# Windowed attention with sinks and a squared-relu layer on one core: order of the first scores, who masks them, and who turns one x

## The chip, the cores and the metric

The kernel runs on one core of a Trainium2 chip. A core has five engines that run side by side and wait for each other through semaphores: TensorE (PE, matmuls and transpositions, writes to PSUM), VectorE (DVE), ScalarE (ACT), GpSimd (POOL) and SyncE (SP, which issues DMAs here; POOL and ACT issue some too). PSUM is used as four score-sized banks, so an operation of TensorE may wait for a bank. The metric is the device time of one execution in microseconds. Before the change it is 226.25 us in the median of four runs (225.96 to 226.46).

## The reference

```python
scores = scale * np.matmul(q, k.transpose(0, 1, 3, 2))       # (4, 8, 768, 768), head_dim 64
keep = is_sink | in_window                                   # first 4 keys; 0 <= i - j < 128
scores = np.where(keep, scores, -1000000000.0)
a = np.exp(scores - np.max(scores, axis=-1, keepdims=True))
a = a / (np.sum(a, axis=-1, keepdims=True) + 1e-09)
attn_out = np.matmul(a, v)
x = attn_out.transpose(0, 2, 1, 3).reshape(B * S, H * D)     # (3072, 512)
h = x @ w_in                                                 # (3072, 2048)
out = np.maximum(h, 0.0) ** 2 @ w_out                        # (3072, 512)
```

## The kernel before

There are four batches of 768 tokens. A batch is cut into three s of 256 tokens (s = 0, 1, 2) and six tiles t of 128; its eight heads go in four pairs m. For each batch attention makes x, layer 1 (`layer1`, L684 to L711) multiplies it with w_in and squares the relu, layer 2 (`layer2`, L714 to L774) multiplies with w_out and stores.

**Attention** (`attention`, its inner `stage`). In batches 0 and 1 SP loads fp32 queries and keys (`qr`, L348), in two groups of tokens: g = 0 holds tokens 0 to 511, g = 1 the last 256. They are cast and regrouped to `qs` (`regroup`), turned by TensorE into PSUM (`transpose`, pt, L476) and copied to `qkT` by VectorE and ScalarE (`unload`). Batches 2 and 3 (`NATURAL`) are cast by POOL's loads (`qn`, L380) and turned by DMA transposes on SP (L436). For each s, `scores` (ps) multiplies a block of 128 keys with up to 256 queries in the window; ScalarE takes the exponential (`expo`, expm, L590); a mask removes what lies outside the window; `values` (po, L634) multiplies with v, whose 65th column sums the weights, and adds the sinks (`es`, `vs`); `norm` divides (L645, L646) into `xn_sb`; `bridge` turns the result by TensorE (px, L671) and a copy makes `xT`. In batches 2 and 3 that turn is made by two DMA transposes per s on SP (`turn_x`, L657) instead.

**Masks.** Three ways stand in the code. With `biased` (batch 0 and s < `BIASED` = 2) TensorE first writes a bias of -30000 outside the window into the bank, as a product with the identity (`bias0` for s = 0, `bias` for s = 1, L564), and adds the scores to it, so that the exponential gives zero. Otherwise VectorE multiplies expm with a 0/1 tile (`mask0` for s = 0, `mask` for the rest, L599), or POOL cuts triangles. `mask` and `mask0` are copied together from two triangles `tri` by POOL (`build_masks`, L252).

**Order.** The order of each engine is not that of the source. Every operation is handed to a planner (`Plan`) with a key, a cost for each engine that may do it, and what it follows; the planner puts them one after the other by earliest start and then key, and the program is written in that order. Each engine then runs its own in order. Costs, `PE_SLACK`, the `margin` of a DMA, and the keys (`at(...)`, `LO`, `HI`) only steer this order. DMAs on one queue are issued in their order; `behind` makes an issue wait for the landing of a named load. SP issues batch 0's first queries and keys (pairs 0 to 3, key before query), the last ones of batch 0 behind the landing of the first part of w_out, and batch 1's behind batch 0's last v. POOL issues v, the four parts of w_in, w_out, later v and the `qn` loads. PSUM banks come from two pools, `att` and `den`, of two each; layer 1 and layer 2 take from `den` alone. `warm` fills expected waits of TensorE in the first 34 us with dummy transpositions (L201).

Around the change TensorE runs, in batch 0: transpositions, then the scores of s = 0 and s = 1 in turns by pair, the four values, both turns of x, and then the eight blocks of layer 1 (four blocks of features, s = 0 and s = 1 in turns). In batch 1 it takes s = 2 first, then s = 0 and s = 1.

Of the kernel before, what the change touches and what calls it, by code (L numbers as in the profile page):

```python
# [14 lines left out]
ALU = mybir.AluOpType  # L15

LATENCY = 0.2
PE_SLACK = 0.334
DMA_START = {"sp": 1.2, "act": 1.2, "pool": 1.6}
DMA_LATENCY = 0.9  # L20
WARM_UNTIL = 34.0
# [112 lines left out]
def kernel(  # L134
# [11 lines left out]
    nc = tc.nc  # L146
# [102 lines left out]
        nc.gpsimd.tensor_copy(out=bias0, in_=bias)  # L249
        nc.gpsimd.memset(bias0[0:NSINK, 1:3, :], 0.0)  # L250

    def build_masks(e):  # L252
        for h2 in range(2):
            for i in range(2):
                nc.gpsimd.tensor_copy(out=mask[:, h2, 2 * i:2 * i + 2, :], in_=tri)
                nc.gpsimd.tensor_copy(out=mask0[:, h2, 2 * i:2 * i + 2, :], in_=tri)
            nc.gpsimd.memset(mask0[0:NSINK, h2, 1:3, :], 1.0)

    def build_head_rows(e):

# [6 lines left out]

    c_fill = op(-9, {"dve": 2.5}, fill)
    c_ident = op(-9, {"pool": 0.3}, build_ident)
    c_tri = op(-0.15, {"pool": 0.6}, build_triangles)  # L270
    c_bias = op(-8, {"pool": 1.3}, build_bias)
    c_sinks = op(-7, {"pool": 0.5}, build_head_rows)


    loaded = {}
# [92 lines left out]
    def load_natural(b, s, older_values):  # L368

        begun = [ops["layer1", b - 2, 0, 0], w_out_op[3]]  # L370
        for ti in (1, 0):
            if s == 0:
                qn_slot[b, ti] = Slot("qr", NT)
            for i in range(2):
                t = 2 * s + i

                def run(e, t=t, ti=ti):
                    if t == 0:
                        qn_t[b, ti] = work["qr"].tile([128, NT, DM], BF16, name="qn", tag="qr")
                    return [nc.gpsimd.dma_start(  # L380
                        out=qn_t[b, ti][:, t, :].rearrange("p (h d) -> p h d", d=D),
                        in_=(q, k)[ti][b, :, 128 * t:128 * t + 128, :].rearrange("h p d -> p h d"))]
                o = dma_op("pool", ("qk", b, ti, t), run, 64 * 0.032,
                           None,
                           [qn_slot[b, ti]] if t == 0 else ())
                o.after += begun
                o.margin = 1.661
        for t in (2 * s, 2 * s + 1):
            def run(e, t=t):
                return [nc.gpsimd.dma_start(  # L390
                    out=v_sb[b % 2][:, t, :, 0:D],
                    in_=v[b, :, 128 * t:128 * t + 128, :].rearrange("h p d -> p h d"))]
            o = dma_op("pool", ("v", b, t), run, 64 * 0.032)
            o.after += begun + older_values
            o.margin = 1.661

    def load_sinks(queue, b):
        eng = nc.scalar if queue == "act" else nc.sync
# [3 lines left out]
    def attention(b, key):  # L402
# [16 lines left out]
        def stage(g, f0, f1, side):  # L419
# [4 lines left out]
            def at(f):  # L424
                return key(f0 + (f1 - f0) * f)
# [3 lines left out]
            if b in NATURAL:  # L429
                for s in range(NS):  # L430
                    for ti in (1, 0):
                        for i in range(2):
                            t = 2 * s + i

                            def turn(e, s=s, ti=ti, i=i, t=t):
                                nc.sync.dma_start_transpose(  # L436
                                    out=qkT_sb[:, :, ti, t, :], in_=qn_t[b, ti][:, t, :])
                            ops["turn", b, ti, t] = op(
                                at(0.1 * s), {"sp": 1.25}, turn, dma=0.3, reads=[qn_slot[b, ti]],
                                after=[ops["qk", b, ti, t]] + prev_scores + prev_sinks)  # L440
                            ops["turn", b, ti, t].margin = 5.167
                            copies.append(ops["turn", b, ti, t])
                    ops["cast", b, s] = ops["v", b, 2 * s + 1]
            w = 2 if n == 2 else 1
# [100 lines left out]
            for s in range(t0 // 256, last // 256):  # L545
# [3 lines left out]
                for m0 in (0, 2):  # L549
# [24 lines left out]
                                        rhs=qkT_sb[r, m, 0, qb:qb + w // 128, :],  # L574
                                        start=(i == 0 and not biased), stop=(i == len(segs) - 1))
                    sc = []
                    for ms in ((m0,), (m0 + 1,)) if b == 0 else ((m0, m0 + 1),):
                        sc.append(op(
                            at(fm), {"pe": len(ms) * (0.7 if biased else 0.28) + 0.1}, lambda e, f=scores, ms=ms: f(e, ms),
                            takes=[banks[m - m0] for m in ms],  # L580
                            after=[ops["turn", b, ti, t] for ti in (0, 1)
                                   for t in range(max(0, 2 * s - 1), 2 * s + 2)] if b in NATURAL else
                            [c for m in ms for gg in range(g + 1) for c in ops["copies", b, m, gg]]))
                        ops["scores", b, s, ms[0]] = sc[-1]
                    masked = []
                    o = 0 if s else 128
                    for j, m in enumerate((m0, m0 + 1)):
# [19 lines left out]
                        if biased:  # L607
                            masked.append(ex)
                            continue
                        first = b == 0 and s < 2  # L610
                        masked.append(op(at(fm + 0.03), {"pool": 1.3} if first else
                                         {"pool": 1.3, "dve": 0.7} if s else {"dve": 0.58, "pool": 1.1},
                                         domask, after=[ex] if first else [ex, late["masks"]]))

                    bo = Slot(side, 1)

# [37 lines left out]
                if b in NATURAL or b == 1 and s in TURNED:  # L654
                    for t in (2 * s, 2 * s + 1):
                        def turn_x(e, t=t):
# [146 lines left out]
    load_v(1, 1, None, ())  # L803
    load_v(1, 2, None, ())

    LO, HI = 0.12, 0.624
    for b in range(B):
        if b == 0:
            at = attention(0, lambda f: f - 1.0)
            at(0, 0.0, 1.0, ("den", "att"))  # L810
            late["masks"] = op(0.006, {"pool": 3.0}, build_masks, after=[c_tri, ops["bridge", 0, 1]])
            at(1, 0.2, 0.725, "att")
        if b == 0:
            for i in range(4):
                for s in range(2):
                    layer1(b, 0.083 * i + 0.042 * s, range(4 * i, 4 * i + 4), 256 * s, 256, (s,))
        else:
            for i, fb in enumerate(range(0, NFB, 2)):
                layer1(b, b + 0.34 * i / 8, (fb, fb + 1), 0, 512, (0, 1))
        for i, fb in enumerate(range(0, NFB, 4)):  # L820
            if b == 0:
                layer1(b, 0.2 + 0.226 * i / 4, range(fb, fb + 4), 512, 256, (2,))
            else:
                layer1(b, b + 0.34 + 0.167 * i / 4, range(fb, fb + 4), 512, 256, (2,))
        if b + 1 < B:
            if b + 1 in NATURAL:
                for s in range(NS):
                    load_natural(b + 1, s, [o for x, o in ops.items() if x[0] == "values" and x[1] == b - 1])
            if b == 0:
                at = attention(1, lambda f: f)  # L830
                at(0, 0.179, 0.751, ("att", "den"))
                at(1, 0.369, 0.369, ("att", "den"))
            else:
                attention(b + 1, lambda f, b=b: b + LO + (HI - LO) * f)(0, 0.0, 1.0, "att")
        for u in range(NS):
            if b == 0 and u < 2:
                layer2(b, u, lambda i, part, u=u: 0.408 + 0.466 * (4 * part + 2 * u + i) / 24, by_part=True)
# [38 lines left out]
```

The softmax here doesn't subtract the row's maximum and nothing guards it: scores larger than these inputs give would overflow.

## Time and profile before

| | us |
|---|---|
| median of four runs | 226.25 |
| the profiled execution, its own time | 226.46 |
| its span | 224.8 |
| TensorE busy | 217.7 |
| VectorE, ScalarE, POOL busy | 103.7, 115.7, 64.8 |
| first matmul of layer 1 | 20.22 |
| granted TensorE clock, all of the span | 1.00 |

A page has the busy time and count of each engine, the chain of work that ended last, and groups of equal instructions. PE is TensorE's matmuls, PEld its weight loads, POOLq, SPq and ACTq the issuing of DMAs. In the list of waits the columns are who waited, for whom, us in total, times, longest. The chain in order of time has start, length and what it was. A row of windows has the length, and for each engine its busy time and number of instructions, then the granted clock, the DMA share and GB/s. The answer for one tile has duration in ns (least, median, most), first and last start in us, and the time from issue to landing of its DMAs. A matmul's duration overlaps the next one's, so a group's length is taken from start to start. Durations of VectorE, ScalarE and TensorE that the prediction uses are the means of groups on the page with shapes kept apart, and starts are from the list of instructions in time.

### The profile page before, as it was taken

What the parts mean: (1) busy time and instruction counts of PE and PEld (TensorE: products, weight loads), DVE (VectorE), ACT (ScalarE), POOL (GpSimd) and SP (SyncE); (2) the same over time, 40 slices, a digit from 0 to 9 for tenths busy, and PEclk for the clock granted to TensorE, in tenths of its full rate; (3) what the DMA queues carried; (4) which work ended last, traced back from release to release, by engine and by line L of the source; (5) the groups of instructions that cost most, each with busy time, mean ns of one, the idle gap of its engine ahead of it and who ended that gap; (6) DMA issues with size and microseconds to landing.
All of it is one profiled execution on the core that took longest, in us unless ns stands there. A gap on an engine that the chain in (4) does not pass through costs nothing.

```text
span 224.8 us, 4606 instructions
## 1 busy us (share of the span) xinstructions
PE 217.7 (97%) x1952; PEld 138.4 (62%) x1952; DVE 103.7 (46%) x192; ACT 115.7 (51%) x131; POOL 64.8 (29%) x99
## 2 busy tenths in 40 slices
PE   7999999998999999999999999999999999999993
PEld 7649995556865796545454645598454455874441
DVE  6736346455855775466462536657241024430010
ACT  2795665514884486377636278665351065551010
POOL 7991015045999424997300000000000000000000
PEclk9999999999999999999999999999999999999999
DMA  6999968997999999999999454020221320000222
GB/s 186 258 176 207 210 191 112 210 326 229 103 200 155 121 206 135 118 157 198 156 131 155 138 158 55 0 50 0 47 96 25 117 96 0 0 3 0 93 98 90
DMA packets 84309, 28.13 MB, mean 125 GB/s; under 512 B 70336, under 2 KB 80832, under 8 KB 84288
## 3 DMA queue, kind: packets, MB, share of 16 engines
q0 software_dynamic: 52608, 10.49, 60.2%
q1 hardware_dynamic: 31496, 17.20, 35.4%
q8 instruction: 15, 0.25, 0.5%
q10 hardware_dynamic: 184, 0.14, 0.2%
q14 instruction: 6, 0.05, 0.1%
HBM read 27.30 MB, written 6.29 MB: 149 GB/s over the span
## 4 chain that ended last, share of the span: by engine, by line
PE 80%; DMA 11%; ACT 2%; SPq 2%; DVE 1%; issue 1%; POOL 1%; POOLq 0%; ACTq 0%
PE pm L694 34%; PE py L734 32%; DMA qr<-in_k_dram 9%; PE po L634 6%; PE ps L571 5%; DMA v<-in_v_dram 3%; SPq L348 2%; PE px L671 1%; PE ps L564 1%; ACT r L703 1%; PE pt L476 1%; ACT expm L590 1%; PE pk L531 0%; POOL v L361 0%; DVE gT L710 0%
## 5 line engine op out<-in xcount | busy, mean ns | idle before, releaser
L734 PE MATMUL py<-w_out_sb,gT 128*128 128x512 bf16 x384 | 88.5, 379 | 0.0
L694 PE MATMUL pm<-xT,w_in_sb 128*128 128x256 bf16 (+1 forms) x576 | 86.7, 308 | 0.4 <-ACT r L703 0.3
L694 PEld LDWEIGHTS <-w_in_sb 128*128 128x128 bf16 x576 | 63.0, 114 | 20.9 <-issue 1.7
L703 ACT ACTIVATE r<-pm 128x1024 bf16<-128x1024 f32 x48 | 49.2, 1025 | 32.8 <-PE pm L694 25.5
L734 PEld LDWEIGHTS <-gT 128*128 128x128 bf16 x384 | 35.4, 98 | 39.2 <-issue 1.7
L710 DVE TENSOR_TENSOR gT<-r 128x1024 bf16<-128x1024 bf16 x48 | 33.1, 690 | 49.5 <-ACT r L703 49.4
L590 ACT ACTIVATE expm<-ps 128x1024 bf16<-128x1024 f32 (+1 forms) x48 | 43.2, 952 | 17.1 <-PE ps L571 17.1
L599 DVE TENSOR_TENSOR expm<-expm,mask 128x1024 bf16<-128x1024 bf16 (+1 forms) x39 | 25.3, 654 | 23.7 <-ACT expm L590 23.2
L206 ACT ACTIVATE osb<-py 128x1024 f32<-128x1024 f32 x9 | 9.2, 1022 | 30.8 <-PE py L734 30.7
L634 PEld LDWEIGHTS <-expm 128*128 128x128 bf16 x352 | 16.5, 97 | 4.1 <-issue 0.6
L634 PE MATMUL po<-v,expm 128*128 128x65 bf16 x352 | 17.5, 193 | 0.0
L646 DVE TENSOR_TENSOR xn_sb<-po,rc 128x512 bf16<-128x512 f32 x24 | 16.6, 691 | 0.8
L571 PE MATMUL ps<-qkT 64*128 64x128 bf16 (+1 forms) x256 | 14.7, 238 | 0.0
L571 PEld LDWEIGHTS <-qkT 64*128 64x128 bf16 x256 | 8.0, 94 | 10.7 <-issue 9.9
L634 PE MATMUL po<-vs,es 128*128 128x65 bf16 x128 | 13.1, 193 | 0.0
L390 POOL DMA_DIRECT2D v<-in_v_dram x12 | 10.7, 914 | 6.0 <-DMA qn<-in_q_dram 5.9
L208 DVE COPY osb<-py 128x1024 f32<-128x1024 f32 (+2 forms) x4 | 3.6, 889 | 19.0 <-PE py L734 15.9
L210 POOL CAST qs<-qr 128x512 bf16<-128x512 f32 x6 | 4.1, 692 | 28.4 <-DMA qr<-in_q_dram 16.0
L208 DVE CAST qs<-qr 128x512 bf16<-128x512 f32 x16 | 7.9, 501 | 8.5 <-DMA qr<-in_k_dram 6.3
L634 PEld LDWEIGHTS <-es 128*128 128x128 bf16 x128 | 11.7, 97 | 0.0
L380 POOL DMA_DIRECT2D qn<-in_q_dram x12 | 10.8, 920 | 2.2 <-DMA qn<-in_k_dram 2.1
L361 POOL DMA_DIRECT2D v<-in_v_dram x12 | 11.0, 937 | 0.6 <-DMA qr<-in_k_dram 0.6
(51 smaller groups left out, 109.9 us busy)
## 6 DMA issues: line engine op xcount, KB each, us to landing
out_dram<-osb SPq DMA_DIRECT2D x11, 512.0 KB, 2.8
v<-in_v_dram POOLq DMA_DIRECT2D x24, 128.0 KB, 6.5
qr<-in_k_dram SPq DMA_DIRECT2D x8, 256.0 KB, 5.1
qr<-in_q_dram SPq DMA_DIRECT2D x8, 256.0 KB, 5.3
w_in_sb<-in_moe_w_in_dram POOLq DMA_DIRECT2D x4, 512.0 KB, 9.3
w_out_sb<-in_moe_w_out_dram POOLq DMA_DIRECT2D x4, 512.0 KB, 10.8
qn<-in_k_dram POOLq DMA_DIRECT2D x12, 128.0 KB, 7.2
qn<-in_q_dram POOLq DMA_DIRECT2D x12, 128.0 KB, 10.1
```

Of the source, the lines that this page charges most:

```text
L208: nc.vector.tensor_copy(out=dst, in_=src)
L361: return [nc.gpsimd.dma_start(out=v_sb[b % 2][:, t, :, 0:D], in_=v[b, :, 128 * t:128 * t + 128, :].rearrange("h p d -> p h d"))]
L380: return [nc.gpsimd.dma_start(out=qn_t[b, ti][:, t, :].rearrange("p (h d) -> p h d", d=D), in_=(q, k)[ti][b, :, 128 * t:128 * t + 128, :]. ...
L571: nc.tensor.matmul(ps[:, h2, o:o + w], lhsT=qkT_sb[r, m, 1, c, :], rhs=qkT_sb[r, m, 0, qb:qb + w // 128, :], start=(i == 0 and not biased) ...
L590: nc.scalar.activation(out=x[:, :, o:512], in_=bank_t["s", b, s, m][:, :, o:512], func=AF.Exp, scale=scale)
L599: nc.vector.tensor_mul(x[:, :, o:512], x[:, :, o:512], mk[:, :, o:512])
L634: nc.tensor.matmul(pv[:, i, h2, :], lhsT=lhsT, rhs=rhs, start=(n_ == 0), stop=(n_ == len(mms) - 1))
L646: nc.vector.tensor_tensor(out=xn_sb[:, 2 * s:2 * s + 2, 128 * m0:128 * m0 + 256].rearrange("p i (j h d) -> p j i h d", j=2, d=D), in0=pv[: ...
L694: nc.tensor.matmul(pm[:, i, :], lhsT=w_in_sb[:, fb // 4, kb, fb % 4:512:4], rhs=xT[:, c0 // 256:(c0 + cw) // 256, kb, :], start=(kb == 0), ...
L703: nc.scalar.activation(out=r, in_=bank_t.pop(tag), func=AF.Relu)
L710: (nc.vector if e == "dve" else nc.gpsimd).tensor_mul(gT_sb[c0 // 512][:, fbs[0]:fbs[0] + n, c0 % 512:c0 % 512 + cw], r, r)
L734: nc.tensor.matmul(pm[:, i, :], lhsT=gT_sb[t // 4][:, fb, 128 * (t % 4):128 * (t % 4) + 128], rhs=w_out_sb[:, fb, :], start=(fb == 0), sto ...
```

## The change

- `BIASED` 2 to 1: in batch 0, s = 1 has no bias matmuls; its four expm are masked by VectorE with `mask`.
- `FIRST`: the scores of s = 1 in batch 0 come after the scores of pairs 2 and 3 of s = 0. (`SINGLE` = 3 keeps one operation for each pair in all of batch 0.)
- `build_masks` is split. `mask` is built by VectorE ahead of its first cast; `mask0` stays on POOL. The triangles are built earlier on POOL.
- `TURNED` = (2,): batch 1's last x (s = 2) is turned by two DMA transposes on SP.
- The first v load waits for the first key load in place of the first query load; w_in waits for the seventh load on SP (keys of pair 3).
- Keys, margins and `PE_SLACK` are changed, and with them the order.

As built, TensorE's order in batch 0 becomes: scores of s = 0, scores of s = 1, values of s = 0, its turn of x, first values of s = 1, layer 1 blocks 0 and 1 of s = 0, second values of s = 1, block 2 of s = 0, turn of x for s = 1, block 3 of s = 0, then the four blocks of s = 1. Layer 2 then does parts 0 to 2 of tiles 0 and 1, parts 0 to 2 of tiles 2 and 3, and the parts 3 with batch 1's first transpositions between. Batch 1 goes s = 0, 1, 2. On SP the two new transposes stand before and after the fourth query transpose of batch 2. Dummy matmuls are 75 instead of 72.

```diff
-PE_SLACK = 0.334
+PE_SLACK = 0.308
...
-    def build_masks(e):
+    def build_mask(e):
+        eng = nc.vector if e == "dve" else nc.gpsimd
         for h2 in range(2):
             for i in range(2):
-                nc.gpsimd.tensor_copy(out=mask[:, h2, 2 * i:2 * i + 2, :], in_=tri)
-                nc.gpsimd.tensor_copy(out=mask0[:, h2, 2 * i:2 * i + 2, :], in_=tri)
-            nc.gpsimd.memset(mask0[0:NSINK, h2, 1:3, :], 1.0)
+                eng.tensor_copy(out=mask[:, h2, 2 * i:2 * i + 2, :], in_=tri)
+
+    def build_mask0(e):
+        eng = nc.vector if e == "dve" else nc.gpsimd
+        for h2 in range(2):
+            for i in range(2):
+                eng.tensor_copy(out=mask0[:, h2, 2 * i:2 * i + 2, :], in_=tri)
+            eng.memset(mask0[0:NSINK, h2, 1:3, :], 1.0)
...
-    c_tri = op(-0.15, {"pool": 0.6}, build_triangles)
+    c_tri = op(-8.5, {"pool": 0.6}, build_triangles)
...
+    c_mask = op(-6, {"dve": 0.65, "pool": 1.6}, build_mask, after=[c_tri])
...
-                o.margin = 1.661
+                o.margin = 1.542
...
-                            ops["turn", b, ti, t].margin = 5.167
+                            ops["turn", b, ti, t].margin = 4.673
...
-                    for ms in ((m0,), (m0 + 1,)) if b == 0 else ((m0, m0 + 1),):
+                    for ms in ((m0,), (m0 + 1,)) if b == 0 and s < SINGLE else ((m0, m0 + 1),):
...
-                            [c for m in ms for gg in range(g + 1) for c in ops["copies", b, m, gg]]))
+                            [c for m in ms for gg in range(g + 1) for c in ops["copies", b, m, gg]] +
+                            ([ops["scores", b, 0, x] for x in FIRST[m0]] if b == 0 and s == 1 else [])))
...
-                        first = b == 0 and s < 2
-                        masked.append(op(at(fm + 0.03), {"pool": 1.3} if first else
-                                         {"pool": 1.3, "dve": 0.7} if s else {"dve": 0.58, "pool": 1.1},
-                                         domask, after=[ex] if first else [ex, late["masks"]]))
+                        masked.append(op(at(fm + 0.03), {"pool": 1.3, "dve": 0.7} if s else {"dve": 0.58, "pool": 1.1},
+                                         domask, after=[ex, c_mask if s else late["mask0"]]))
...
-                        o_.margin = 2.284
+                        o_.margin = 2.623
...
-    NATURAL, TURNED, BIASED = (2, 3), (), 2
+    NATURAL, TURNED, BIASED, SINGLE = (2, 3), (2,), 1, 3
+    FIRST = {0: (2, 3), 2: (2, 3)}
...
-    load_v(0, 0, ("qk", 0, 0, 0, 0))
+    load_v(0, 0, ("qk", 0, 0, 1, 0))
...
-        load_w_in(i, None if i == 0 else None)
+        load_w_in(i, ("qk", 0, 3, 1, 0) if i == 0 else None)
...
-    LO, HI = 0.12, 0.624
+    LO, HI = 0.087, 0.413
...
-            late["masks"] = op(0.006, {"pool": 3.0}, build_masks, after=[c_tri, ops["bridge", 0, 1]])
-            at(1, 0.2, 0.725, "att")
+            late["mask0"] = op(-0.01, {"pool": 1.8, "dve": 0.8}, build_mask0, after=[c_tri, ops["bridge", 0, 1]])
+            at(1, 0.2, 1.5, ("att", "den"))
...
-                layer1(b, b + 0.34 * i / 8, (fb, fb + 1), 0, 512, (0, 1))
+                layer1(b, b + 0.276 * i / 8, (fb, fb + 1), 0, 512, (0, 1))
...
-                at(0, 0.179, 0.751, ("att", "den"))
-                at(1, 0.369, 0.369, ("att", "den"))
+                at(0, 0.056, 0.1, ("att", "den"))
+                at(1, 0.497, 0.344, "att")
```

More of the change, by code (lines that the diff above doesn't have):

```diff
@@ L394, in load_natural @@
             o.after += begun + older_values
-            o.margin = 1.661
+            o.margin = 1.542
     def load_sinks(queue, b):
@@ L818 @@
             for i, fb in enumerate(range(0, NFB, 2)):
-                layer1(b, b + 0.34 * i / 8, (fb, fb + 1), 0, 512, (0, 1))
+                layer1(b, b + 0.276 * i / 8, (fb, fb + 1), 0, 512, (0, 1))
         for i, fb in enumerate(range(0, NFB, 4)):
             if b == 0:
-                layer1(b, 0.2 + 0.226 * i / 4, range(fb, fb + 4), 512, 256, (2,))
+                layer1(b, 0.269 + 0.295 * i / 4, range(fb, fb + 4), 512, 256, (2,))
             else:
-                layer1(b, b + 0.34 + 0.167 * i / 4, range(fb, fb + 4), 512, 256, (2,))
+                layer1(b, b + 0.276 + 0.167 * i / 4, range(fb, fb + 4), 512, 256, (2,))
         if b + 1 < B:
@@ L836 @@
             if b == 0 and u < 2:
-                layer2(b, u, lambda i, part, u=u: 0.408 + 0.466 * (4 * part + 2 * u + i) / 24, by_part=True)
+                layer2(b, u, lambda i, part, u=u: 0.392 + 0.479 * (4 * part + 2 * u + i) / 24, by_part=True)
             else:
```

## The prediction

> **What bounds the kernel now.** I read the page's busy shares and chain first, then all waits of TensorE, then the chain in order of time, then the one stretch in which TensorE never stops, then the loads that the new order needs earlier.
>
> ```profile
> span 224.8 us, 4606 instructions
> PE 217.7 (97%) x1952; PEld 138.4 (62%) x1952; DVE 103.7 (46%) x192; ACT 115.7 (51%) x131; POOL 64.8 (29%) x99
> PE 80%; DMA 11%; ACT 2%; SPq 2%; DVE 1%; issue 1%; POOL 1%; POOLq 0%; ACTq 0%
> ```
> ```profile
> PE pt L201 <- POOL ident L239: 1.5, 1, 1.5
> PE pt L476 <- ACT qkT L206: 1.0, 1, 1.0
> PE pm L694 <- ACT r L703: 0.3, 1, 0.3
> PE ps L201 <- ACT expm L590: 0.2, 1, 0.2
> ```
> TensorE is busy 97% of the span and waits four times, 3.0 us in all, so a gain has to come from less TensorE work or from those waits. But busy time also counts dummy matmuls (`warm`, L201) in the first 20 us. Where work really waits is in the chain:
>
> ```profile
> 19.66 0.53 PE px L671 x8
> 20.20 0.02 issue
> 20.22 5.41 PE pm L694 x48
> ...
> 35.46 5.97 DMA v<-in_v_dram
> ...
> 42.49 8.99 DMA qr<-in_k_dram
> 51.48 0.02 issue
> 51.50 0.43 DVE qs L208
> 51.93 0.61 DVE qkT L208
> 52.54 0.02 issue
> 52.56 0.61 ACT qkT L206
> 53.17 0.04 issue
> 53.21 0.65 PE pt L476 x8
> ```
> Layer 1 starts at 20.22. At 53.21 TensorE has just waited 1.0 us for a cast that waited for the second key load of batch 1 (landed 51.48). That load goes back over batch 0's last v load (35.46 to 41.43) and POOL's and SP's issues to the loads of the weights: a chain of transfers, in which no attention or layer work stands. After it:
>
> ```profile
> 53.21:220.87 167.66, 167.30 (x1400) 100.99 (x1399) 74.80 (x129) 86.94 (x96) 41.90 (x51) 1.00 0.95 99
> ```
> This is one window's row: length 167.66, TensorE 167.30 busy (0.34 is the third wait), clock 1.00. From 53.2 on the time is TensorE's work; before, it is the transfers.
>
> **The change, part by part.**
> *Masks of tokens 256 to 511 of batch 0.* Eight bias matmuls of 128x512 go (pairs take 0.43 to 0.54 in the chain: 2.0 us); four VectorE multiplications of 128x1024 come (0.70 each). All of it lies before 53.2, so the 2.0 us count only as far as TensorE isn't waiting for the load at its end.
>
> *First scores ahead.* ScalarE now decides when layer 1 can start: behind its last key cast (9.0 to 9.6) stand four exponentials of 128x768 (0.81), two copies of 0.60, one of 0.38, three exponentials of 128x1024 (1.02) and the copy of the first x (1.02): 8.9 us, so 18.5, and 18.6 with one wait; overlap of neighbours could take 0.9 off, waits add 1. The masks for the first values end at 17.4 and hide behind it. Layer 1 then starts about 1.6 earlier, but holds one block of values (0.73) and one transposition (0.45) in its midst, so its eight blocks (1.75 each) end at 33.8 against 34.19. It needs the four parts of w_in in its first four blocks: the fourth is issued at 12.2, takes 12.2 and lands at 24.3; its block starts at 25.0. That is 0.7 of slack, so a still earlier start gives nothing.
>
> *Load order.* The first v load waits for a key load instead of the query load, but POOL reaches it only at 6.08, behind the sink products: nothing moves. w_in now waits for the seventh load on SP (3.99 plus 4.93: 8.92); POOL reaches it at 9.96. Cost 0, with 1.0 of cover; nothing waits behind it but w_out.
>
> *Masks built on VectorE.* Four copies of 128x256 ahead of the first casts. No row shows one: VectorE's fill of the same size (0.27) and POOL's copy (0.40) are nearest. I take 0.27 (same engine), 1.1 in all; at 0.40 it is 1.6, at nothing 0. The first two casts end at 5.5 to 6.0 instead of 4.9; the dummies hold TensorE until 5.74. 0 to 0.3, taken up by ScalarE's chain and the load at 51.48.
>
> *The wait at 53.* TensorE now comes to batch 1's first transposition at about 48.8, needs the query load that is cast from 48.99 on (49.4), does part 3 of token tiles 0 and 1, and needs at 52.5 and 53.15 the same copies behind the cast of 51.50 (they stand behind it on VectorE in both programs). The pair of scores ends at 53.45. Up to there the early gain is lost: if it had been 1 us smaller, nothing would differ.
>
> *What is left after it.* Against the stretch from 53.21, TensorE has 16 matmuls fewer: one pair of scores (8 in 0.44, and 0.1 of handing over) done already, and the eight transpositions of batch 1's last x (0.45), which go to DMA. 167.32 less 0.97 is 166.35.
>
> *Batch 1 in the order 0, 1, 2.* New: its first values stand seven groups behind 53.45 (1.73 + 3 x 0.45 + 1.75 + 0.33 + 0.54 + 1.75: 60.9), and need v of the second tile. Its load is POOL's second of these:
>
> ```profile
> L361 POOL DMA_DIRECT2D v<-in_v_dram x6: 893/917/961, 56.0 to 60.4; - x6
> DMA to landing us min/median/max: 4.5/4.7/6.4
> ```
> Issued at 56.9 and 4.5 on its way, it lands at 61.5; the values start at 61.55: a wait of 0.65 that the kernel before didn't have, since it began batch 1 with its last tokens. A wait of 0.35 for a score bank ahead of it (a relu of 1.02 behind a matmul block that ends at 58.3) lies inside. Least 0, if other waits already cost as much; most 1.9, if the load takes the 6.4 of the slowest.
>
> *VectorE between 55 and 68.* It gets masks, casts and copies of batch 1 closer together: some 23 operations of 0.5 to 0.7, 12 to 13 us in 13. The second values need masks that end at 65.8 by this count and TensorE comes at 67.2: 0 up to a slip of 1.4.
>
> *Last x of batch 1 by DMA.* Two transposes on SP (1.22 each, 2.5 to land), issued near 84 and 86. Their reader in layer 1 stands near 98. What is behind them on SP is five transposes of batch 2's keys and queries: the first of these is issued at about 86 and lands 6.2 to 9.0 later (the same ones before), at 92.5 to 95; its scores stand at 95. 0, at most 1.
>
> The Trainium skill (VectorE: DVE Perf Modes, The three transpose paths) gives 390 ns for 128x128 on TensorE and 1309 ns by DMA, and advises TensorE if PSUM can take the result. On its figures eight tiles would cost about 7 us more, by estimate, and the sum would be that much worse if they lay on the path. The row of 1.22 per issue of four tiles says less, and with the reader 10 us away it isn't on the path.
>
> *The sum.* 53.45 + 166.35 + 0.65 = 220.45, against 220.87 for TensorE's end; the tail behind it is the same. The profiled execution took 226.46, so 226.04; it was 0.21 above the median of the runs, so 225.8.
>
> **Rivals.**
> 1. *No wait for v.* If the 0.65 is not there (v lands earlier, or TensorE is held elsewhere anyway), the end is 219.8, 225.2; with 0.65 of the wait at 53 gone as well (TensorE ready at 51.9), 224.5. For it: the stretch after 53 ran with 0.34 of waits before. Against: the load's issue follows a landing (55.46) that compute doesn't move.
> 2. *Slower: the second store falls onto the v loads.* The first two results leave in 53 to 57 instead of at 54.10 and near 60. In the trace v loads took 4.5, but the two issued around the store of 60.0 took 5.6 and 6.4. Now that store is issued at about 56.5, amid v's first two. At +1.1 to +1.9 on 61.5 each tenth is TensorE's: 226.9 to 227.7. It decides from +0.9 (226.7). Against: the store of 54.10 left the loads of 56.0 at 4.5, and POOL issues one only every 0.87, so a short overlap is made good.
>    The Trainium skill (DMA: Bandwidth & Descriptors, Queues, rings and completion order) says that each DMA engine takes turns between rings packet by packet, which speaks for this rival; the rows of 5.6 and 6.4 agree.
> 3. *The early part moves nothing at all*, and the wait for v and the saved work cancel: 226.0 to 226.3.
> 4. *Batch 2's transposes late behind the two new ones* on SP: 0.5 to 1.5 at 95: 226.3 to 227.3.
> 5. *The DMA chain itself moves earlier* (w_in and v disturb the first loads less): what it moves comes off whole, up to 1 us: 224.8.
>
> **How the numbers follow.** Chances: forecast 0.50 (its own range 225.2 to 226.4, a little over half of it under 225.8), rival 1 0.15, rival 2 0.17, rival 3 0.06, rival 4 0.05, rival 5 0.07. About 0.2%, or 0.45 us, is what a measurement tells from no change. Faster: 0.28 of the forecast, rivals 1 and 5: 0.50. Same: 0.20 of the forecast, rival 3: 0.26. Slower: 0.02 of the forecast and rivals 2 and 4: 0.24. The range for 8 in 10 runs from rival 1's low end to inside rival 2: 224.5 to 227.2.
>
> **What would show it.** Layer 1 (pm) starts between 18 and 19.6, its four first blocks without a wait for w_in; no matmul on `bias`. TensorE stands idle about 1 us in all between 48 and 53.5, the last of it behind VectorE's cast of the load that lands near 51.5. The first po of batch 1 starts at 61.5, released by DMA v. Behind it no wait of TensorE over 0.3. Wrong if layer 1 starts after 20, if the key load lands more than 0.5 from 51.5, if v's second load takes over 5.4, or if pm of batch 1's last tokens or ps of batch 2 are released by a DMA transpose.

## The result, and the profile after

The changed kernel is slower: its time is 1.0055 of the kernel before (95% interval 1.0039 to 1.007). With 226.08 us before, over 56 executions in the same sessions, that is 227.3 us; the prediction was 225.8, with 224.5 to 227.2 as its range. Ten of the changed kernel's 36 executions, all over 228.9 us, count as a slow state and are left out of this ratio; the median with them is 227.8 us. The profiled execution took 227.52 us, its span is 225.8.

First the page of the changed kernel: the span, the busy time of each engine, and the chain's shares by engine.

```profile
span 225.8 us, 4587 instructions
PE 215.3 (95%) x1939; PEld 137.1 (61%) x1939; DVE 105.0 (46%) x199; ACT 115.1 (51%) x132; POOL 63.4 (28%) x94
PE 73%; DMA 15%; POOL 5%; DVE 2%; SPq 1%; issue 1%; ACT 0%; POOLq 0%
```

TensorE is busy 2.4 us less than before (215.3 against 217.7, dummies included) and the span is 1.0 longer: it stands idle 3.4 us longer, 1.8 of them in the first 18.7 us, ahead of layer 1, and the rest behind. In the chain, DMA and POOL went from 12% to 20%. The waits of TensorE behind 18 us (who waited, for whom, us in total, times, longest):

```profile
PE po L640 <- DMA v<-in_v_dram: 1.4, 1, 1.4
PE pm L700 <- DMA w_in_sb<-in_moe_w_in_dram: 1.1, 1, 1.1
PE pm L700 <- ACT r L709: 0.5, 1, 0.5
```

The 1.0 us for the cast at 53 is gone. In its place stand 1.1 us for w_in in layer 1 and 1.4 us for v at the first values of batch 1, with 0.5 for a score bank just ahead of it. The chain in order of time (start, length, what) shows where these two loads hang:

```profile
6.91 3.65 POOL v L368 x4
10.57 2.90 POOL w_in_sb L307 x4
13.46 15.52 DMA w_out_sb<-in_moe_w_out_dram
...
44.36 0.74 PE po L640 x24
45.13 0.22 DVE rc L651
45.37 0.69 DVE xn_sb L652
46.06 0.12 DVE rc L651
46.21 0.69 DVE xn_sb L652
46.90 0.69 DVE qs L208
47.65 0.37 SPq L355
48.07 6.88 DMA qr<-in_k_dram
54.99 0.50 issue
55.48 0.95 POOL v L368
56.44 6.61 DMA v<-in_v_dram
63.09 0.46 PE po L640 x10
```

Read the lower part from its end. The values resume at 63.09, when batch 1's second v load lands. It was issued at 56.44 and took 6.61 us. POOL could issue the first v load only when a key load had landed (48.07 plus 6.88); SP could issue that one only when VectorE had cast `qs` and so freed a buffer; and VectorE came to that cast late because it divided batch 0's values, which TensorE had made at 44.36. So the landing of v isn't a fixed point in time: in this execution it hangs on TensorE's own work in batch 0.

One row of windows, from the resumption to TensorE's end (length, then busy time of PE, PEld, DVE, ACT, POOL, granted clock, DMA share, GB/s):

```profile
63.09:221.99 158.90, 158.87 (x1306) 94.56 (x1305) 65.09 (x113) 78.26 (x84) 32.59 (x40) 1.00 1.02 95
```

TensorE is busy 158.87 of 158.90 us. Whatever delays the values at 63.09 delays the end by as much.

Last, the loads and stores at this place: the answer for tile v (the issues' duration, first and last start, then us from issue to landing), and that for out_dram.

```profile
L368 POOL DMA_DIRECT2D v<-in_v_dram x6: 893/908/1111, 55.5 to 60.1; - x6
...
DMA to landing us min/median/max: 5.4/6.8/7.0
```
```profile
L756 SPq DMA_DIRECT2D out_dram<-osb x2: 377/382/387, 54.3 to 56.6; - x2
```

Before, the same six loads took 4.5/4.7/6.4 us, and the second store left near 60:

```profile
L750 SPq DMA_DIRECT2D out_dram<-osb x2: 378/383/388, 54.1 to 60.0; - x2
```

Now it leaves at 56.6, and the data queues show what it does two to three microseconds later (packets, MB, share of the 16 engines; q0 is POOL's loads, q1 SP's store). First the microsecond from 59 to 60, then that from 60 to 61:

```profile
q1 hardware_dynamic: 169, 0.33, 91.5%
q0 software_dynamic: 57, 0.01, 11.4%
```
```profile
q0 software_dynamic: 1044, 0.13, 207.4%
q1 hardware_dynamic: 26, 0.04, 11.4%
```

While the store moves its 0.33 MB, the v loads get 57 packets through instead of 1044 (1166 in the microsecond from 59 on of experiment 1, where the store is held).

### The profile page after: what moved, and what is told of

Read it like the earlier page. It is cut to its first block, busy times and chain, and to the rows that moved or that the text cites. A ratio compares the mean times of both kernels' runs of the same rounds, so it can differ in the third digit from the quotient of the medians.

```text
span 225.8 us, 4587 instructions
## 1 busy us (share of the span) xinstructions
PE 215.3 (95%) x1939; PEld 137.1 (61%) x1939; DVE 105.0 (46%) x199; ACT 115.1 (51%) x132; POOL 63.4 (28%) x94
## 3 DMA queue, kind: packets, MB, share of 16 engines
q0 software_dynamic: 52608, 10.49, 68.5%
## 4 chain that ended last, share of the span: by engine, by line
PE 73%; DMA 15%; POOL 5%; DVE 2%; SPq 1%; issue 1%; ACT 0%; POOLq 0%
PE py L740 33%; PE pm L700 30%; DMA w_out_sb<-in_moe_w_out_dram 7%; PE po L640 5%; PE ps L578 4%; DMA qr<-in_k_dram 3%; DMA v<-in_v_dram 3%; DMA qr<-in_q_dram 2%; POOL v L368 2%; POOL w_in_sb L307 1%; SPq L355 1%; POOL vs L521 1%; DVE qs L208 1%; DVE xn_sb L652 1%; PE pk L538 0%
## 5 line engine op out<-in xcount | busy, mean ns | idle before, releaser
L700 PE MATMUL pm<-xT,w_in_sb 128*128 128x256 bf16 (+1 forms) x576 | 87.9, 309 | 1.6 <-DMA w_in_sb<-in_moe_w_in_dram 1.1
L740 PE MATMUL py<-w_out_sb,gT 128*128 128x512 bf16 x384 | 87.6, 379 | 0.0
L607 DVE TENSOR_TENSOR expm<-expm,mask 128x1024 bf16<-128x1024 bf16 (+1 forms) x43 | 27.8, 653 | 13.8 <-ACT expm L598 13.0
L206 ACT ACTIVATE osb<-py 128x1024 f32<-128x1024 f32 x10 | 10.3, 1027 | 39.8 <-PE py L740 39.8
L640 PE MATMUL po<-v,expm 128*128 128x65 bf16 x352 | 18.1, 193 | 1.5 <-DMA v<-in_v_dram 1.4
L651 DVE RECIPROCAL rc<-po 128x8 f32<-128x8 f32 x24 | 4.9, 206 | 21.4 <-PE po L640 21.2
L208 DVE COPY osb<-py 128x1024 f32<-128x1024 f32 (+2 forms) x3 | 2.3, 780 | 20.8 <-PE py L740 17.7
L387 POOL DMA_DIRECT2D qn<-in_k_dram x12 | 10.7, 904 | 4.4 <-DMA v<-in_v_dram 4.2
L208 DVE CAST qs<-qr 128x512 bf16<-128x512 f32 x17 | 8.4, 502 | 7.3 <-DMA qr<-in_q_dram 3.9
```

Source lines behind the costliest of these rows:

```text
L208: nc.vector.tensor_copy(out=dst, in_=src)
L607: nc.vector.tensor_mul(x[:, :, o:512], x[:, :, o:512], mk[:, :, o:512])
L640: nc.tensor.matmul(pv[:, i, h2, :], lhsT=lhsT, rhs=rhs, start=(n_ == 0), stop=(n_ == len(mms) - 1))
L700: nc.tensor.matmul(pm[:, i, :], lhsT=w_in_sb[:, fb // 4, kb, fb % 4:512:4], rhs=xT[:, c0 // 256:(c0 + cw) // 256, kb, :], start=(kb == 0), ...
L740: nc.tensor.matmul(pm[:, i, :], lhsT=gT_sb[t // 4][:, fb, 128 * (t % 4):128 * (t % 4) + 128], rhs=w_out_sb[:, fb, :], start=(fb == 0), sto ...
```

## The experiments

All ratios are to the kernel before, with their 95% intervals. Two theories stood from the start. A: the second store takes v's place, v lands late, and TensorE's end moves with it. B: v is late anyway. Theories C and D are on the other wait, that for w_in: swallowed later (C), or coming through to the end (D).

**1. The store out of the way.**

```diff
-            nc.sync.dma_start(out=..., in_=bank_t.pop(("osb", b, u)))
+            d = nc.sync.dma_start(out=..., in_=bank_t.pop(("osb", b, u)))
+            if b == 0 and u == 1:
+                after_dma(d, loaded["v", 1, 1])
```

> The changed kernel with one more wait: the second output store of batch 0 (issued at 56.6 us in the changed kernel) is held on SP until batch 1's second v load has landed. No other instruction moves. Theory A (the store takes the v loads' place in the DMA engines): the load issued at 56.44 takes 4.5 to 5.4 us instead of 6.6 and lands at 61.0 to 61.9, TensorE's wait for v falls from 1.40 to 0.4 or less, and the end comes 1.0 to 1.4 us earlier: 0.9990 to 1.0015 of the kernel before instead of 1.0055. Theory B (v is late by itself or by the loads ahead of it): the load still takes about 6.6 us and the ratio stays at 1.0055.

Measured: 0.9992 (0.9966 to 1.0018), 1.4 us less than the changed kernel. The answers for v and for the store, and the waits of TensorE behind 18 us:

```profile
L368 POOL DMA_DIRECT2D v<-in_v_dram x6: 893/908/1111, 54.8 to 59.4; - x6
...
DMA to landing us min/median/max: 3.7/5.2/5.5
```
```profile
L756 SPq DMA_DIRECT2D out_dram<-osb x2: 378/383/388, 53.5 to 60.7; - x2
```
```profile
PE pm L700 <- ACT r L709: 0.5, 1, 0.5
PE po L640 <- ACT r L709: 0.3, 1, 0.3
PE pm L700 <- DMA w_in_sb<-in_moe_w_in_dram: 0.2, 1, 0.2
```

The second v load was issued at 55.70 and landed at 60.67, 5.0 us instead of 6.6, and no matmul waits for v. (That it was issued 0.7 earlier than in the trace of the changed kernel isn't the edit's doing.) One wait on one DMA gives back the loss; B falls. In this execution w_in also came in time (a wait of 0.2), which the edit can't have caused: it differs from one execution to the next.

**2. Both stores on v.** The same edit with `u == 0` and `loaded["qk", 1, 2, 0, 1]` in place of `loaded["v", 1, 1]`, so that the first store comes later instead.

> The changed kernel with the first output store of batch 0 held from 54.29 us to the landing of batch 1's last query load (about 55.7), so that both stores are issued amid the first v loads. Theory A (stores delay v): the first and second v load take longer still, the second 7.5 to 8.5 us, TensorE's wait for v grows from 1.40 to 2.3 to 3.3 us and the end comes 0.9 to 1.9 later: 1.0095 to 1.014 of the kernel before. Theory B (v is late by something else): nothing moves, 1.0055.

Measured: 1.0129 (1.0093 to 1.0165), 1.7 us more than the changed kernel. TensorE's wait for v, and the answer for the six v loads of batch 1:

```profile
PE po L640 <- DMA v<-in_v_dram: 2.9, 2, 1.7
```
```profile
DMA to landing us min/median/max: 7.4/8.6/8.7
```

The dose works in the other direction too: two stores there, a second load of 8.4 us, 2.9 us of waiting.

The trace holds a second cost behind that wait. Here is the window of the next layer 1 block (16 matmuls), first in this kernel, then in the changed one; the third figure from the end is the granted clock:

```profile
65.80:69.28 3.48, 3.48 (x18) 2.59 (x19) 2.55 (x5) 1.27 (x2) 3.03 (x4) 0.53 3.22 147
```
```profile
64.59:66.52 1.93, 1.93 (x19) 1.92 (x20) 1.90 (x5) 1.27 (x2) 1.92 (x3) 1.00 2.72 151
```

The block took 3.48 us instead of 1.93, at a clock of about half. The traces of experiments 8 and 9, which waited 2.3 and 1.8 us for v, show the same: a clock of 0.50 for 3.4 us, from 0.8 us after the values resume, and 1.4 us lost by it (1.7 here). The traces that waited 1.6 us or less for v don't show it. The profiled executions of experiments 2, 8 and 9 have a mean clock of 0.992 or 0.993 over the span. So have 5 of the 6 executions here, 13 of the changed kernel's 36 (229.4 us in the mean, against 227.2 for the other 23), one of 12 in experiment 1, and none of those of the kernel before that the ratios use. A late v thus seems to cost twice in about a third of the changed kernel's executions: the wait, and slower work behind it. No trace of the changed kernel at this clock was kept, and no run varied the wait alone, so this link is read from the traces and not shown by an experiment.

**3. The same store on the same loads in the kernel before.** The edit of experiment 2 in the kernel before.

> The kernel before with the first output store of batch 0 held from 54.10 us to the landing of batch 1's last query load (56.25), so that it lies on the first v loads of batch 1 as the second store does in the changed kernel. Theory A (a store beside the v loads delays them by 1.5 to 2 us, and it costs only because the changed kernel begins batch 1 with its first tokens and needs v two us after its issue chain allows): the second v load takes 6.0 to 7.0 us instead of 4.5 and lands at 63.0 to 64.0 instead of 61.49, but no matmul waits for it, and the ratio is 0.999 to 1.0015. Theory K (late v loads cost in either order, through the batch 2 loads queued behind them on POOL): the ratio rises to 1.004 or more.

Measured: 1.0013 (0.9996 to 1.0031). The store was issued at 54.54 between the first two v loads; the answer for the six v loads reads

```profile
DMA to landing us min/median/max: 6.2/6.2/7.6
```

against 4.5/4.7/6.4 in the kernel before. The second load took 6.16 us. The landing I expected, 63.0 to 64.0, was missed (61.38), since in this execution v was issued 1.7 us earlier (54.26) than in the trace of the kernel before. No matmul waits for v. So K is out, and the store's collision alone costs little or nothing; it costs in the changed kernel because that one needs v in tiles 0 and 1 first, at about 61.5, where the kernel before reads v of batch 1 from 67.8 on.

**4. v issued earlier.**

```diff
-                    after_dma(d, loaded[behind])
+                    after_dma(d, loaded[("qk", 1, 2, 0, 0) if name == ("v", 1, 0) else behind])
```

> The changed kernel with the first v load of batch 1 issued behind the landing of the query load two before (the last one of the first four tiles' query and key loads of batch 1) instead of the key load of the last tokens. In the changed kernel POOL issues it at 55.48 when a key load lands at 54.95; that earlier load lands near 52. POOL would issue v from about 52.6 on, three us earlier. Theory A (the second v load is late because a store lies on it): the second load is issued at 53.5, three us ahead of the second store, shares the queues with the last key and query loads and the first store, and lands at 59 to 61: the wait for v is gone, 0.999 to 1.0015. Theory B (v needs 6 to 7 us in any case): it lands near 60, the wait is gone too, so this run alone doesn't tell A from B, but it tells whether the wait for v is what costs the time: if it goes and the ratio stays at 1.0055, it isn't.

Measured: 0.9979 (0.9953 to 1.0005). POOL gained less than the three microseconds I counted on: it issued v from 53.89 instead of 55.48, the second load at 54.84. That load took 7.8 us, because now both stores (54.77 and 57.09) lay on it, and it landed at 62.65, only 0.4 earlier. TensorE came to these values at 61.95 instead of 61.47, since it had waited 1.7 us for w_in, and so the wait for v was 0.5 instead of 1.4. The profiled execution took 227.09 us, the most of the twelve (median 225.4), so it shows less than the ratio: starting earlier helps by 1.7 us, and how, this trace tells only in part.

**5. The sink products on VectorE.** POOL then reaches its loads earlier.

```diff
-                        (nc.vector if e == "dve" else nc.gpsimd).tensor_tensor(
+                        (nc.vector if e == "dve" or b == 0 else nc.gpsimd).tensor_tensor(
                             out=vs[32 * j:32 * j + 32, 2 * j:2 * j + 2, :],
```

> The changed kernel with the four sink products of batch 0 made by VectorE (behind the mask copies, ahead of the casts) instead of POOL, which so reaches its loads of v about 2.1 us earlier (4.75 instead of 6.86) and those of w_in about 1.3 us earlier (9.2, held by the seventh load). Theory C (what is lost before 53 us is swallowed by the wait for the key load of batch 1): w_in's fourth part lands at 24.5 to 25.5, the wait of 1.09 for it falls under 0.3, layer 1 ends about 1 us earlier, TensorE then waits about as much longer for batch 1's second key load, and the time stays within 0.3 us of the changed kernel: 1.004 to 1.007. Theory D (the early 1.09 us come through to the end): 1.0005 to 1.001.

Measured: 0.9987 (0.9961 to 1.0013), 1.5 us less than the changed kernel. TensorE's waits hold no w_in any more, and of v only

```profile
PE po L640 <- DMA v<-in_v_dram: 0.2, 1, 0.2
```

The fourth part of w_in landed at 24.87 instead of 26.55. C fell. D's 1.0005 to 1.001 lies inside the interval, but both had taken the landing of v for fixed; it came at 60.32 instead of 63.05, because everything of the chain shown above came earlier: TensorE made batch 0's values at 42.78 instead of 44.36, and POOL issued the first v load at 53.50 instead of 55.48.

**6. The mask copies later on VectorE.** `c_mask` does nothing, and `build_mask("dve")` is called at the head of `sink_keys` of batch 0.

> The changed kernel with VectorE's four mask copies moved from 3.5 us to behind its last copies of keys and queries (about 11 us, ahead of the sink keys), so that they no longer run beside POOL's fills and sink products. Theory E (POOL is slower while VectorE makes the mask copies and casts behind them): POOL's fill of 4x256 takes 0.30 again instead of 0.45, its four sink products 1.9 instead of 2.16, and it reaches v at 6.3 to 6.5 instead of 6.86; the w_in wait shrinks by about 0.4, and the ratio, 1.0055 for the changed kernel, falls to 1.002 to 1.005, unless the copies at 11 us push layer 1 back by as much. Theory F (only the triangle's new place on POOL makes it late: 0.28 us of waiting for its fill): POOL's durations and 6.86 stay, and the ratio is 1.0055 or higher.

Measured: 1.0052 (1.0022 to 1.0082). First POOL's instructions in time for the changed kernel (start, length, line, operation), then for this one:

```profile
3.69 0.45 POOL L250 MEMSET bias<- 4x256 bf16 x1
...
4.75 2.16 POOL L521 TENSOR_TENSOR vs<-vs_in,head_rows 32x130 bf16<-32x130 f32 x4
6.86 3.71 POOL L368 DMA_DIRECT2D v<-in_v_dram  x4
```
```profile
3.71 0.30 POOL L250 MEMSET bias<- 4x256 bf16 x1
...
4.67 1.86 POOL L523 TENSOR_TENSOR vs<-vs_in,head_rows 32x130 bf16<-32x130 f32 x4
6.47 3.71 POOL L368 DMA_DIRECT2D v<-in_v_dram  x4
```

On POOL, E is right for the fill alone. It takes 0.44 or 0.45 in all the traces of the changed kernel and of edits that leave VectorE's mask copies (3.5 to 4.3) beside it, and 0.30 here and in the kernel before. The four products don't tell: with the mask copies in place they took 2.16 in this trace of the changed kernel, but 1.93 in experiment 4 and 1.86 in experiment 8, and without them 2.13 in experiment 3. In the changed kernel's trace the last and longest of them (0.65) starts at 6.26, just behind a cast on VectorE that starts at 6.23; when a cast starts is set by the landing of its load. So of the 0.78 us by which POOL came later in that trace, some 0.3 is the triangle's new place (POOL waits 0.25 for the fill of `tri` at 1.45), 0.15 the fill, and 0.3 the products, which differ between executions. The Trainium skill (SBUF — State Buffer, Who interferes with whom) has a rule for this: VectorE's copies and casts can take the port pair that GpSimd uses too, and the later one waits for the whole instruction. The row of the fill agrees with it; which of VectorE's instructions took the port, it doesn't show.

The time decides nothing between E and F: the interval holds E's 1.002 to 1.005 and F's 1.0055. w_in landed at 25.43, its wait went, and layer 1 ended at 34.24 instead of 35.35. But v's second load landed at 62.63, only 0.4 earlier than in the changed kernel, and the waits for v were 1.6: what had been gained was waited away there. (Layer 1 began at 19.08 instead of 18.70; its chain goes back to the last query load, cast at 10.49 instead of 10.12, so that the moved copies needn't have a share in it.)

**7. The sink products on VectorE in the kernel before.** The edit of experiment 5.

> The kernel before with the four sink products of batch 0 made by VectorE instead of POOL, so that POOL reaches its first v load at about 4.3 instead of 6.08 us. Theory G (as predicted from the profile of before, the wait of TensorE at 53 hangs on a chain of transfers that begins with POOL's issues): the second key load of batch 1 is cast 1.0 to 1.8 us earlier than 51.50, the wait of 1.0 at 53 falls under 0.3, and the time falls by 0.7 to 1.0 us: 0.9955 to 0.997. Theory H (the chain is set by the amount moved and not by when POOL begins): the cast stays within 0.3 of 51.50 and the ratio is 0.999 to 1.001.

Measured: 1.0014 (0.9996 to 1.0032): neither G's gain nor H's unmoved chain. TensorE's waits, and one row of windows:

```profile
PE pk L531 <- DVE kblk L508: 0.8, 1, 0.8
PE pt L476 <- DVE qs L208: 0.6, 2, 0.5
PE pm L694 <- ACT r L703: 0.3, 1, 0.3
```
```profile
53.07:220.54 167.47, 167.12 (x1403) 101.01 (x1400) 74.10 (x128) 86.94 (x96) 41.39 (x50) 1.00 0.98 99
```

The wait of 1.0 at 53 went, as G says. But VectorE's extra 1.3 us ahead of the casts held up the attention of batch 0, and layer 1 started at 21.59 instead of 20.22. The transposition that stood at 53.21 now stands at 53.07. Against the trace of the kernel before, 1.37 us lost at layer 1 cost nothing, since the wait behind it went by about as much. But that wait isn't in every execution. Experiment 3 has the instructions of the kernel before up to 54 us, and in its trace VectorE makes the cast of 51.50 at

```profile
49.68 0.43 DVE L208 CAST qs<-qr 128x512 bf16<-128x512 f32 x1 [0.84 <-DMA qr<-in_k_dram]
```

and TensorE doesn't wait at 53 at all (225.07 us). So whether POOL's earlier issues made the key load earlier here can't be told from this one trace, and the ratio says only that the two effects of the edit together come to about nothing.

**8. The waits of the first loads put back.**

```diff
-            if behind is not None:
+            if behind is not None and name != ("w_in", 0):
                 for d in ds:
-                    after_dma(d, loaded[behind])
+                    after_dma(d, loaded[behind if name != ("v", 0, 0) else ("qk", 0, 0, 0, 0)])
```

> The changed kernel with the waits of its first loads put back: the first v load waits for batch 0's first query load and w_in for none, as in the kernel before. The prediction's step (POOL comes to both later than what they wait for, so these waits cost nothing): POOL issues v at 6.6 to 6.9 and w_in at 10.3 to 10.6 as in the changed kernel, and the ratio stays at 1.004 to 1.007. Rival L (they are what makes w_in land late): w_in issued 0.5 us or more earlier, its wait gone, ratio 1.003 or lower.

Measured: 1.0067 (1.0035 to 1.0099), POOL at v at 6.56 and at w_in at 10.40. It comes to v 0.30 earlier than in the trace of the changed kernel because its products took 1.86 instead of 2.16, not because of the waits; TensorE still waited 1.0 us for w_in. The new load order does nothing in the changed kernel, and L is out. (In experiment 5, where POOL comes to w_in sooner, it did wait 0.5 us for the seventh load.)

**9. Batch 1's last x turned by TensorE again.** `TURNED` is `()`.

> The changed kernel with batch 1's last x turned by TensorE again (8 transposes and one copy) instead of two DMA transposes; the planner also moves some of batch 1's later work. Theory I (as predicted, the DMA turn is hidden and saves TensorE its 8 transposes): TensorE works 0.4 to 0.6 us longer behind 66 us, the ratio goes from 1.0055 to 1.007 to 1.0085. Theory J (the two transposes on SP cost as much by delaying batch 2's): no wait disappears in the profile, or the ratio is 1.0055 or lower.

Measured: 1.0078 (1.0045 to 1.011). That is 0.5 us above the changed kernel, as I expected for 8 transpositions more, but the interval also holds 1.0055: the DMA turn is a gain of about this size or none, and nothing here makes it a part of the loss. The trace of this execution shows something else. w_in came without a wait, TensorE was at the values of batch 1 at 59.8, 1.7 us earlier than in the trace of the changed kernel; v was issued 1.9 us earlier, but its second load took 7.2 us. The wait was 1.8, and the clock behind it fell as in experiment 2. With the store where it is, being early in layer 1 was turned into waiting for v.

**10 and 11. Hold and sinks together, and with the earlier v.** The edits of 1 and 5, then those of 1, 4 and 5.

> The changed kernel with both: the second store of batch 0 held until batch 1's second v load has landed, and batch 0's sink products on VectorE. With the sink products alone the profile kept a wait for v of 0.2 us and none for w_in, at a ratio of 0.9987; with the hold alone none for v and 0.2 for w_in, at 0.9992. Theory A+D (the waits for v and for w_in are two separate losses, and both come through to the end): neither wait is left, TensorE waits under 1.0 us in all between 18 us and the end, and the ratio is 0.993 to 0.997. Theory C (the early part is swallowed, the sink products helped only by bringing v earlier, so that hold and sinks remove the same loss): no better than one of them, 0.998 to 1.0.

> The changed kernel with all three: second store held behind batch 1's second v load, batch 0's sink products on VectorE, and the first v load of batch 1 behind an earlier landing. With the first two the profile has left TensorE waits of 0.2 and 0.5 us near 59 and none for v. Theory A+D: nothing is left for the earlier v to remove, 0.993 to 0.998. Rival M (in executions other than the profiled one v is still late now and then): the scatter shrinks and the ratio falls to 0.990 to 0.994. Rival N (earlier v loads take the last key and query loads' time): 0.998 or more.

Measured: 0.9954 (0.9931 to 0.9976) and 0.9957 (0.994 to 0.9973). What is left of TensorE's waits behind 18 us with hold and sinks:

```profile
PE pm L700 <- ACT r L709: 0.5, 1, 0.5
PE ps L578 <- ACT qkT L206: 0.2, 1, 0.2
PE po L640 <- ACT r L709: 0.2, 1, 0.2
```

This is what A and D expected: both edits together come out below either alone, though the intervals touch (0.9931 to 0.9976 against 0.9966 to 1.0018 and 0.9961 to 1.0013). They don't add up in full (1.4 and 1.5 us alone, 2.3 together), since the sink products had already taken most of the wait for v. That the second loss is the wait for w_in is likely and not shown: the sink products bring all later loads earlier too, and the trace of experiment 1 had only 0.2 of that wait. Issuing v earlier on top brings nothing; in that run it was issued at 51.27 and landed long before it was needed. The version with hold and sinks is 0.46% faster than the kernel before, 1.0 us, and 2.3 us faster than the changed kernel. So the new order of work was worth something, and late transfers took it back: the one for v for certain, the one for w_in probably.

## Why the prediction was wrong

The likeliest case was wrong, and rival 2 was the one that happened, at its own price: it gave 226.9 to 227.7 for a second v load that lands 1.1 to 1.9 us behind 61.5; it landed 1.55 behind it, and the time is 227.3 us. I gave it 0.17. With the clock of experiment 2 the wait costs still more in some executions; neither the forecast nor the rival had that.

- **The step that failed: "Batch 1 in the order 0, 1, 2".** It counted on 4.5 us for the second v load and a landing at 61.5, so 0.65 of waiting, with the 0.35 for the bank inside it. It took 6.6 and landed at 63.05. The waits were 0.5 for the bank and 1.4 for v, 1.9 in all, the most that I had allowed. The forecast put TensorE's end at 220.45 and it came at 221.99; of these 1.54 us, 1.26 are this term (1.91 against 0.65), and the rest is the start of the stretch (0.12) and the work in it (0.16).
- **What I gave against rival 2 was wrong twice.** I wrote that the store of 54.10 had left the loads of 56.0 at 4.5. That store's data were over before theirs moved (its queue had one packet in the microsecond from 57 on, where v began); the store of 56.6 moves its data at 59 to 60, in the middle of v's. And I wrote that a short overlap is made good, as POOL issues a load only every 0.87. The trace shows that the loads were already backed up: all six took 5.4 to 7.0.
- **Rival 1's "against" held one false statement that mattered to the forecast too:** that the issue of v follows a landing "that compute doesn't move". The chain after shows compute in it (values, division, cast, buffer, key load, v). In experiments 5 and 9, which were earlier at the end of layer 1, v was issued 2.0 and 1.9 us earlier; in experiment 6 the chain went over two key loads instead, and v stayed at 55.44.
- **"First scores ahead": layer 1 from 18.6.** Measured 18.70. Right. But "the fourth lands at 24.3, 0.7 of slack" was wrong: it landed at 26.55, its block waited 1.09, and the eight blocks ended at 35.35 instead of 33.8. It was issued at 12.7 instead of 12.2, and took 13.8 us; the duration of 12.2 was one sample.
- **"Masks built on VectorE": 0 to 0.3.** The four stand from 3.51 to 4.29, 0.8 us in all for the 1.1 taken. What was missing is POOL. I placed it at 6.08 and 9.96 by its times of before; it came at 6.86 and 10.53, by the triangle's new place, by the fill beside the mask copies, and by sink products that took 0.3 longer in that execution (experiment 6).
- **"Load order": nothing moves.** Right as an effect (experiment 8), though the two times it named were not.
- **"The wait at 53": the early gain is lost there.** Not so in the profiled execution: the key load landed at 50.85 and not at 51.5, TensorE came to this place 1.6 us later than I had counted (50.42 for 48.8), without waiting, and the pair of scores ended at 53.57 for the predicted 53.45. The number was right for another reason, the wait for w_in, and so by luck. In the kernel before, too, the wait at 53 is in one trace and not in another (experiment 7); I had taken it for fixed.
- **"What is left after it", 166.35.** From 53.57 to 221.99 are 168.42 us; less the waits of 1.91 that is 166.51. Right.
- **"VectorE between 55 and 68" and "last x by DMA": 0.** Right: behind 63.09 TensorE stands idle for 0.03 us. The two transposes landed 6.5 us after their issue and not 2.5, at 92.7 and 95.3; their reader stands at about 100.
- **The numbers.** Faster 0.50 rested on a store whose data I placed by its issue alone. The range ended at 227.2, inside rival 2, and the time fell 0.1 beyond it, or 0.6 with all executions counted.

## What to carry to other kernels

When a change moves a consumer closer to its load, look at everything else that will be in the DMA queues while that load moves, by when its data move and not by when it is issued; a store that nobody waits for is the cheapest thing to hold back. A load's issue time is seldom fixed: follow its chain through buffers and waits back to the engine that frees them before taking it as an anchor. A transfer with 0.7 us of slack in one execution can have none in the next. And where TensorE waits longer, look at its granted clock behind the wait as well as at the wait.

## What the runs showed of the hardware

- A store of 512 KB on SP's queue, issued at 56.61, moved its data from about 58.5 to 60.3, and for about a microsecond nearly stopped POOL's loads of 128 KB (57 packets against 1044 in the next microsecond). I had expected a sharing of the engines. Five of the six loads that it met took 6.6 to 7.0 us; with the store held, they took 5.0 to 5.5 (experiment 1).
- Packets of the store were about 2 KB each (0.33 MB in 169), those of the v loads about 125 bytes (0.13 MB in 1044). That fits a turn-taking by packets in which the large ones take most of the time; no run here varied the packet size.
- POOL's fill of 4x256 took 0.45 us instead of 0.30 beside VectorE's mask copies. Its four products took 1.86 to 2.16 us in different executions, with the mask copies and without.
- After TensorE had waited 1.8 to 2.9 us for v, the granted clock was 0.50 for about 3.4 us (experiments 2, 8 and 9); after waits of up to 1.6 us it stayed at 1.00 (the changed kernel, experiments 4 and 6).
- The same load differs between executions: TensorE waited 1.1, 0.2, 1.7 and 0 us for w_in in kernels with the same instructions up to there (the changed kernel, experiments 1, 4 and 9).
